# A parallel attention and MLP block: the second layer norm as a factor, memory products with tokens as rows, the memory update on four column tiles, and a new order

## The chip, the cores and the metric

The kernel runs on one core of a Trainium2 chip. The metric is the device time of one execution in microseconds (us). The engines are named as in the profile: PE multiplies matrices and PEld loads their weights, DVE (VectorE), ACT (ScalarE) and POOL (GpSimd) compute elementwise, and SP issues DMAs.

## The reference

For x of 2048 tokens with 512 features the kernel computes x + A(xn) + B(xn), where xn is the layer norm of x. A is an attention with a compressive memory in 32 heads of 16 features; B is an MLP that takes its own layer norm of xn.

```python
xn = layernorm(x)
# A: four segments of 512 tokens; M and z start at zero; phi(t) = t + 1 if t > 0 else exp(t)
for s in range(4):
    p = softmax(qs @ ks.T * 0.25 + mask)
    a_dot = p @ vs
    a_mem = (phi(qs) @ M) / (phi(qs) @ z + 1e-6)
    o_s = g * a_mem + (1 - g) * a_dot       # g = sigmoid(beta), one per head
    M = M + phi(ks).T @ vs
    z = z + phi(ks).sum(tokens)
A = concat(o) @ wo
# B: y is a second layer norm of xn
B = gelu(layernorm(xn) @ w1 + b1) @ w2 + b2      # w1: 512 x 1792, w2: 1792 x 512
```

The mask takes out the keys with a higher index than the query. Because xn has mean zero, the second norm only scales each token: layernorm(xn) is xn times one factor per token, 1/sqrt(var(xn) + 1e-5).

## The kernel before

The work is cut into 16 units i of attention: segment s = i // 4 and a group g = i % 4 of eight heads, whose 8 x 16 features fill the 128 partitions. The MLP is cut into 16 units j: 256 tokens (hf = j // 2) and one half of w1's 14 column blocks (fh = j % 2, FH = 7 blocks). Weights and activations are split into two f16 halves, and a product is three f16 matmuls per 128 rows (`split3`, L499 to 506).

There is no scheduler at run time and none in the compiler that moves work: `streams()` lists the jobs, `ORDER` (L134) is a string in which each letter takes the next job of one stream, and the program issues the jobs in that sequence; each engine then executes its own instructions in order. `BANKS` (L154) gives each product its PSUM bank out of eight. The two strings are written out in the source. The job keys that matter here:

- `X` and `Xt` (L462, L477, L487): load 128-token tiles of x, take the statistics on DVE (`norm_stats`, L424: one inverse root for both norms, `stats[..., 0, :]` for the first and `stats[..., 1, :]` for the first and second in one), normalise on POOL (L458), transpose on PE (L490, four f32 transposes per tile), and split on ACT and DVE (L493, L494) into `xnT`, one buffer for the 512 tokens of a segment.
- `Y` and `Yt`: the same for the MLP's input: x is loaded again, normalised with the second pair of statistics and transposed into `yT`, one buffer of 256 tokens.
- `T`, `Tv`, `Tw`, `Tr`, `N`: projections of k and q for a unit (L521), their low halves, phi on ACT and DVE (L529, L543 to 549), the way through DRAM (stores `kd`, `qd` at L536 to 538, loads into `kst`, `qst` at L557) that brings eight heads into place, and the transposes of phi(k) (L562). `V`: the values (L608).
- `M`, `R`, `Rr`, `S`, `Sg`, `pv`, `PV`: logits and their row maxima (L646, L653; both on 64-row halves of the array), the maxima through DRAM (L664, L669), logits again and exponentials (L688, L695), the causal cut on POOL (L709), and the products with the values on four column tiles of 32 (L722).
- `K` (`kv`, L616): phi(k) transposed times v for a head group as four 128 x 128 f32 products (L621), of which only the diagonal blocks are kept by a mask (L624 or L628) and added to the memory `mst` on POOL (L629).
- `Z`, `Qd`, `Qe`, `Qn`, `Q`: the read from memory, features as rows. `z_rep` spreads z over a 128 x 128 mask (L581), a product with phi(q) of 512 columns gives the denominator of every feature row (L589), ACT adds 1e-6 (L591), the reciprocal is taken by Ln, Exp and a Newton step (L568, L569, L573, L574), a second product of 512 columns gives the numerator (L601), and L602 multiplies them.
- `O`: the attention's division and the sum with the memory part `ame` (L740 to 759). `out`: the product with wo (L849) into `acc`. `st`: the store.
- `D`: one column block of w1 (L781, twelve matmuls of 256 columns on `yT`); each block's product is scaled and gets b1 from ACT or DVE in turn (`Z_ON`, L784, L786). `G`: gelu over all seven blocks in one ACT instruction of 1792 elements (L791). `H`: splitting h in f16 halves (L801, L803, L805). `e`: the product with w2 (L831).
- `wl`, `wm`, `wf`, `ws`: weight loads, sums of squares, scales and splits, all begun in the first 180 us.

## Time and profile before

| what | value |
|---|---|
| median of 3 runs (lowest to highest) | 720.85 us (720.42 to 723.13) |
| the profiled execution's own time | 720.38 us |
| its span in the trace | 718.7 us |
| PE busy | 689.8 us, 5189 matmuls |
| DVE busy | 524.3 us |
| ACT busy | 519.7 us |
| POOL busy | 352.9 us |
| granted PE clock | 1.0 of full speed |

All rows of the trace stand against the span; what lies around it, 720.38 - 718.7 = 1.7 us, is taken as unchanged. An f32 product counts as two matmuls in the rows. The end of a matmul in the trace lies after the start of the next one, since they overlap: the pace of a stretch is read from the start of one group to the start of the next, and not from the busy time alone.

### The profile page before, as it was taken

The numbers are of one execution on the slowest core, as the hardware profiler recorded it, in microseconds if no ns is written. First come the engines' busy times: TensorE is split into PE (matmuls) and PEld (weight loads), VectorE is DVE, ScalarE is ACT, GpSimd is POOL, SyncE is SP. The second block draws the span as 40 slices with busy tenths as digits, with TensorE's granted clock in tenths as the row PEclk, the third lists the DMA queues.
The fourth block names the chain that finished last, engine by engine and source line by source line (L and its number), as shares of the span: only waits on it lengthen the run. The fifth ranks groups of instructions, "written<-read, shape, count | busy, mean of one in ns | idle before, by whom it ended". The sixth has DMA issues, their size and how long they took to land.

```text
span 718.7 us, 14578 instructions
## 1 busy us (share of the span) xinstructions
PE 689.8 (96%) x5189; PEld 379.0 (53%) x5189; DVE 524.3 (73%) x1677; ACT 519.7 (72%) x908; POOL 352.9 (49%) x544
## 2 busy tenths in 40 slices
PE   2799999999999999999999999999999999999997
PEld 2365655564554465665555456556556455455543
DVE  5799877988786659897485866888658484696642
ACT  5989998889767577578936757676864567748980
POOL 3568746655514462654533336445634245334572
PEclk9999999999999999999999999999999999999999
DMA  9886124503220163322313024322240321322101
GB/s 266 242 255 157 53 79 108 127 16 92 52 68 3 61 148 89 82 53 55 96 31 90 16 66 113 92 60 60 68 104 2 97 67 17 82 68 68 32 1 59
DMA packets 54084, 59.16 MB, mean 82 GB/s; under 512 B 5038, under 2 KB 40892, under 8 KB 54012
## 3 DMA queue, kind: packets, MB, share of 16 engines
q1 hardware_dynamic: 51708, 54.04, 27.0%
q0 software_dynamic: 2304, 4.20, 3.6%
q8 instruction: 41, 0.67, 0.4%
q14 instruction: 31, 0.25, 0.1%
HBM read 41.18 MB, written 17.04 MB: 81 GB/s over the span
## 4 chain that ended last, share of the span: by engine, by line
PE 84%; DMA 5%; ACT 5%; DVE 2%; issue 2%; SPq 1%; POOL 0%; POOLq 0%; DVEq 0%; ACTq 0%
PE dense L505 33%; PE dense L831 19%; PE dense L722 9%; PE dense L646 6%; PE dense L688 5%; PE dense L849 5%; DMA qst<-qd 2%; DMA qd<-hl 2%; PE dense L601 2%; PE dense L589 1%; PE dense L621 1%; PE dense L490 1%; ACT pt L695 1%; DMA pt<-in_A_wq_dram 1%; PE dense L562 1%
## 5 line engine op out<-in xcount | busy, mean ns | idle before, releaser
L653 DVE CUSTOM_DVE_ANT_0 dense<-dense,mask 128x384 f32<-128x384 f32 (+3 forms) x512 | 234.0, 524 | 37.9 <-PE dense L646 35.8
L695 ACT ACTIVATE pt<-dense,qkcs 128x512 f32<-128x512 f32 (+1 forms) x384 | 204.4, 628 | 28.0 <-PE dense L688 27.9
L831 PE MATMUL dense<-w2s,hT 128*128 128x512 f16 x672 | 165.3, 380 | 0.0
L505 PE MATMUL dense<-yT,w1s 128*128 128x256 f16 x1344 | 160.5, 273 | 1.8 <-POOL w1s L413 1.4
L709 POOL TENSOR_SCALAR_AFFINE_SELECT pt<-pt 128x256 f32<-128x256 f32 x256 | 102.7, 443 | 104.5 <-ACT pt L695 104.0
L505 PEld LDWEIGHTS <-w1s 128*128 128x128 f16 x1344 | 129.5, 98 | 34.7 <-issue 9.9
L805 POOL TENSOR_TENSOR hT<-hh,hT 128x512 f16<-128x512 f32 x64 | 69.5, 1086 | 64.6 <-ACT hT L803 61.9
L831 PEld LDWEIGHTS <-hT 128*128 128x128 f16 x672 | 60.9, 98 | 71.3 <-issue 16.7
L722 PE MATMUL dense<-pt,vt 128*32 128x512 f32 (+3 forms) x1024 | 76.3, 436 | 0.0
L653 DVE DVE_READ_ACCUMULATOR2_ANT mc<- 128x1 f32 x512 | 71.9, 140 | 0.0
L801 POOL TENSOR_SCALAR hh<-hT,sc 128x512 f32<-128x512 f32 x64 | 43.4, 679 | 46.7 <-ACT hT L791 43.6
L784 ACT ACTIVATE hT<-dense,b1t,sc 128x256 f32<-128x256 f32 x64 | 36.7, 573 | 37.8 <-PE dense L505 37.3
L753 POOL TENSOR_TENSOR nN<-nN,oT 128x512 f32<-128x512 f32 x16 | 20.5, 1280 | 73.8 <-DVE oT L574 73.8
L646 PE MATMUL dense<-kst,qst 48*128 48x384 f16 (+3 forms) x512 | 52.7, 298 | 3.8 <-DMA qst<-qd 3.8
L722 PEld LDWEIGHTS dense<-pt,vt 128*32 128x32 f32 x1024 | 30.9, 109 | 45.2 <-issue 33.4
L688 PE MATMUL dense<-qst,kst 50*128 50x384 f16 (+3 forms) x512 | 52.1, 298 | 2.1 <-DMA qst<-md 1.7
L505 PE MATMUL dense<-xnT,wks 128*128 128x512 f16 x192 | 45.6, 388 | 0.0
L505 PE MATMUL dense<-xnT,wqs 128*128 128x512 f16 x192 | 44.1, 379 | 0.0
L849 PE MATMUL dense<-wos,oT 128*128 128x512 f16 x192 | 43.8, 379 | 0.1
L505 PE MATMUL dense<-wvs,xnT 128*128 128x512 f16 x192 | 43.6, 379 | 0.0
L803 ACT ACTIVATE hT<-hh 128x512 f16<-128x512 f32 x64 | 37.4, 584 | 7.4 <-POOL hh L801 7.4
L786 DVE TENSOR_SCALAR hT<-dense,sc,b1t 128x256 f32<-128x256 f32 x48 | 25.9, 539 | 23.0 <-PE dense L505 22.8
(223 smaller groups left out, 931.5 us busy)
## 6 DMA issues: line engine op xcount, KB each, us to landing
xt<-in_A_x_dram SPq DMA_DIRECT2D x30, 256.0 KB
kd<-hl SPq DMA_DIRECT2D x48, 128.0 KB
qd<-hl SPq DMA_DIRECT2D x48, 128.0 KB
kst<-kd SPq DMA_DIRECT2D x32, 192.0 KB
qst<-qd SPq DMA_DIRECT2D x32, 192.0 KB
acc<-in_A_x_dram SPq DMA_DIRECT2D x16, 256.0 KB
acc<-in_B_b_dram POOLq DMA_DIRECT2D x16, 256.0 KB, 4.1
out_dram<-acc SPq DMA_DIRECT2D x16, 256.0 KB
```

Source lines behind the costliest of these rows:

```text
L505: T.matmul(p, wsl(ws, k, a), xsl(xs, k, b), start=s0 and i == 0, stop=s1 and i == 3 * n - 1)
L646: T.matmul(p[:, o:o + n], stk[i, 0][r, t, P * qb:P * qb + P], stk[i, 1][r, t, :n], start=True, stop=True)
L653: V.tensor_tensor_reduce(p[:, o:o + n], p[:, o:o + n], mask[:, 512 - n:], 1.0, -3e38, OP.add, OP.max, mc[i][:, 4 * b + t, qb:qb + 1])
L688: T.matmul(p[:, o:o + n], stk[i, 1][r, t, P * kb:P * kb + P], stk[i, 0][r, t, P * kb:], start=True, stop=True)
L695: A.activation(pt[i, 4 * b + t][:, OFF[kb]:OFF[kb] + n], p[:, c:c + n], AF.Exp, scale=qkcs[:, 1, i % NG:i % NG + 1])
L709: G.affine_select(v, v, pattern=[[0, 2], [1, P]], compare_op=OP.is_ge, fill=0.0, base=0, channel_multiplier=-1)
L722: T.matmul(p[32 * c:32 * c + 32, P * kb:], vt[s, kb][:, 4 * g + c, 16 * odd:16 * odd + 32], pt[i, 2 * c + odd][:, OFF[kb]:OFF[kb] + LEN[kb ...
L801: G.tensor_scalar(hht[j, c], hz[:, z, :], col(SHH + j % 2), 0.0, op0=OP.mult, op1=OP.add)
L803: A.activation(hT[:, z, 0, :], hht[j, c], AF.Copy)
L805: G.tensor_tensor(hT[:, z, 1, :], hht[j, c], hT[:, z, 0, :], op=OP.subtract)
L831: T.matmul(p, t[:, u, P * a:P * a + P], w2s[:, fo, v, :], start=fi == 0 and n == 0, stop=fi == FH - 1 and n == 2)
L849: T.matmul(p, o[:, u, P * b:P * b + P], wos[:, g, v, :], start=i == 0, stop=i == 3 * NG - 1)
```

## The change

The second norm's pass over x is gone: `Y` and `Yt` fall away, and with them `yT`. The `D` products read `xnT`, which becomes a ring of three halves of 256 tokens; half h of the eight lies in slot h % 3. The factor of each token is computed from the statistics (`ratio`, key `C`), turned into a row with a DVE transpose, written to DRAM by two DMAs, and brought back to all partitions as a row of 256 factors (`ratio_rows`, key `Cb`, a buffer that each half reuses). `D` fills a bank with two column blocks, and one DVE instruction multiplies both by the scale and the row. b1 moves into gelu, which becomes seven ACT instructions with a bias each.

The memory read swaps its operands: phi(q), 128 tokens at a time, is the weight, and the moving operand `mx` has 128 columns of masked memory and eight of z (`z_cols`, key `Z`). The products have tokens as rows and eight denominators per token (`a_mem`, key `Q`); DVE takes an exact reciprocal and multiplies, and four PE transposes and an ACT copy bring the result back to features as rows (`a_turn`, key `Qt`). `gr` holds the gates of all heads on every partition.

`kv` does sixteen products of 32 x 32 instead of four of 128 x 128, on four column tiles, and adds the 32 columns straight to `mst` on DVE, without a mask and without POOL.

In segment 1 the two halves do not lie side by side in the ring (slots 2 and 0), and `T` there takes 24 matmuls of 256 columns instead of twelve of 512 (`x_seg`). `ORDER` and `BANKS` are new throughout; their strings are left out below. The new sequence starts with the x loads ahead of the first weight loads.

```diff
--- before.py
+++ after.py
...
@@ -66,9 +65,9 @@
         for b in range(2):
             put("norm", *[("X", n, b, k) for k in range(4)] * (n > 0))
             put("normt", *[("Xt", n, b, k) for k in range(2)])
-    for n in range(2 * NSEG):
-        put("again", *[("Y", n, 0, k) for k in (0, 2, 3)])
-        put("againt", *[("Yt", n, 0, k) for k in range(2)])
+    for h in range(2 * NSEG):
+        put("ratio", ("C", h))
+        put("ratio2", ("Cb", h))
...
@@ -97,10 +96,8 @@
             put("heads%d" % k, ("O", i, k))
         if s:
             put("mem0", ("Z", i))
-            put("mem1", ("Qd", i))
-            put("mem2", ("Qe", i))
-            put("mem3", ("Qn", i))
-            put("mem4", ("Q", i))
+            put("mem1", ("Q", i))
+            put("mem2", ("Qt", i))
         if s < NSEG - 1:
             put("nat", ("N", i))
             put("kv", ("K", i))
...
@@ -419,7 +416,9 @@
 
     I_MAGIC = 0x5F3759DF
 
-    stats = cst.tile([P, S // P, 2, 2], F32, name="stats")
+    stats = cst.tile([P, 4, 4, 2], F32, name="stats")
+    G.memset(stats, 0.0)
+    nws = {}
 
     def norm_stats(tok, tiles):
 
@@ -430,28 +429,52 @@
             st = sm.tile([P, 6], F32, name="st")
             V.bn_stats(st, t)
             V.bn_aggr(ag[:, j, :], st)
...
-        for j in range(2):
-            V.scalar_tensor_tensor(r[:, :, j, 1], ag[:, :, 0], -1.0, r[:, :, j, 0], op0=OP.mult, op1=OP.mult)
-
-    def norm_apply(tok, tiles, twice, act, j):
+        for o in range(0, n, 2):
+            r = stats[:, (tok + o) // 2 % 4]
+            V.scalar_tensor_tensor(r[:, 1], ag[:, o:o + 2, 0], -1.0, q[:, o:o + 2, 0], op0=OP.mult, op1=OP.mult)
+            V.tensor_copy(r[:, 0], q[:, o:o + 2, 0])
+
+    cd = [dr.tile([2, 4, 32], F32, name=f"cd{h}") for h in range(2 * NSEG)]
+    ct = cst.tile([P, 4, 4, 2], F32, name="ct")
+    cbt = {}
+
+    def ratio(h):
+
+        w, o = nws[2 * h]
+        a, q = w[:, 0, o:o + 2], w[:, 3, o:o + 2]
+        c = stats[:, h % 4, 2]
+        V.tensor_tensor(c, a[:, :, 0], q[:, :, 0], op=OP.mult)
+        V.tensor_tensor(c, c, q[:, :, 1], op=OP.mult)
+        V.transpose(ct.rearrange("p a b c -> p (a b c)"), stats.rearrange("p a b c -> p (a b c)"))
+        j = 8 * (h % 4) + 4
+        for t in range(2):
+            Q.dma_start(cd[h][t], ct.rearrange("(q j) a b c -> j q (a b c)", j=32)[j + t])
+
+    def ratio_rows(h):
+        cbt[h] = sb.tile([P, 256], F32, name="cb")
+        Q.dma_start(cbt[h], bass.AP(tensor=cd[h].tensor, offset=cd[h].offset, ap=[[0, P], [1, 256]]))
+
+    def norm_apply(tok, tiles, act, j):
         for t in tiles[j:j + 1]:
-            a, b = stats[:, tok + j, twice, 0:1], stats[:, tok + j, twice, 1:2]
+            a, b = (stats[:, tok // 2 % 4, k, j:j + 1] for k in range(2))
             if act:
                 A.activation(t, t, AF.Identity, bias=b, scale=a)
             else:
...
@@ -493,22 +509,29 @@
         A.activation(h, p3, AF.Copy, scale=1024.0)
         V.scalar_tensor_tensor(dst[:, :, 1, c0:c0 + P], p3, 1024.0, h, op0=OP.mult, op1=OP.subtract)
 
...
+    def x_seg(s):
+
+        a, b = 2 * s % 3, (2 * s + 1) % 3
+        if b == a + 1:
+            return [(slice(0, 512), lambda k, u: xnT[:, a:a + 2, k, u, :])]
+        return [(slice(256 * j, 256 * j + 256), lambda k, u, h=h: xnT[:, h, k, u, :]) for j, h in enumerate((a, b))]
+
...
     stk, pkn, ame, pqt = {}, {}, {}, {}
-    bg = cst.tile([P, NG, 5], F32, name="bg")
-    mst = cst.tile([P, NG, P], F32, name="mst")
+    bg = cst.tile([P, NG, 4], F32, name="bg")
+    gr = cst.tile([P, H], F32, name="gr")
+    mst = cst.tile([P, NG, 2 * DH], F32, name="mst")
     zst = cst.tile([P, NG], F32, name="zst")
     zs = {}
 
@@ -518,8 +541,8 @@
         s, g = divmod(i, NG)
         w = (wqs, wks)[which]
         p = dense()
-        split3(p, ((w, lambda w, k, a: w[:, g, a, P * k:P * k + P]),
-                   (xnT[s], lambda t, k, a: t[:, k, a, :])), KT, True, True)
+        for c, xs in x_seg(s):
+            split3(p[:, c], lambda k, a: w[:, g, a, P * k:P * k + P], xs)
...
@@ -573,40 +596,49 @@
         V.tensor_tensor(src, src, tmp, op=OP.mult)
         V.scalar_tensor_tensor(dst, src, 2.0, tmp, op0=OP.subtract, op1=OP.mult)
 
-    zrt = {}
-
-    def z_rep(i):
+    amt, mx = {}, {}
+
+    def z_cols(i):
         g = i % NG
-        zrt[i] = sm.tile([P, P], F32, name="zr", bufs=1)
-        V.tensor_scalar(zrt[i], bd.rearrange("p a b -> p (a b)"), zst[:, g:g + 1], None, op0=OP.mult)
-
-    rden = {}
-
-    def a_den(i, part):
-        if part == 0:
-            g = i % NG
-            p = dense()
-            T.matmul(p, zrt[i], pqt[i, 0], start=True, stop=True)
-            rden[i] = sb.tile([P, 512], F32, name="rc")
-            A.activation(rden[i], p, AF.Copy, bias=1e-6, scale=qkcs[:, 0, g:g + 1])
-        elif part == 1:
-            ame[i] = sb.tile([P, 512], F32, name="ame")
-            log_recip(rden[i], ame[i])
-        else:
-            newton(rden[i], rden[i], ame[i])
+        mx[i] = sm.tile([P, P + GH], F32, name="mx")
+        V.tensor_tensor(mx[i][:, :P].rearrange("p (a b) -> p a b", a=4), mst[:, g, :].unsqueeze(1).to_broadcast([P, 4, 2 * DH]),
+                        bd.rearrange("p (a b) c -> p a (b c)", a=4), op=OP.mult)
+        V.tensor_scalar(mx[i][:, P:], half, zst[:, g:g + 1], None, op0=OP.mult)
 
     def a_mem(i):
         g = i % NG
+        amt[i] = sb.tile([P, 512], F32, name="rc")
+        r = sm.tile([P, 4, GH], F32, name="rd", bufs=1)
+        ps = []
+        for b in range(2):
+            p = dense()[:, :2 * (P + GH)].rearrange("p (t c) -> p t c", t=2)
+            ps.append(p)
+            for t in range(2):
+                T.matmul(p[:, t, :], pqt[i, 0][:, P * (2 * b + t):P * (2 * b + t) + P], mx[i],
+                         start=True, stop=True)
+        c = qkcs[:, 0, g:g + 1]
+        for b, p in enumerate(ps):
+            V.tensor_scalar(r[:, 2 * b:2 * b + 2, :], p[:, :, P:], c, 1e-6, op0=OP.mult, op1=OP.add)
+        V.reciprocal(r, r)
+        V.scalar_tensor_tensor(r, r, c, gr[:, GH * g:GH * g + GH].unsqueeze(1).to_broadcast([P, 4, GH]),
+                               op0=OP.mult, op1=OP.mult)
+        for b, p in enumerate(ps):
+            V.tensor_tensor(amt[i][:, 256 * b:256 * b + 256].rearrange("p (t h e) -> p t h e", t=2, h=GH),
+                            p[:, :, :P].rearrange("p t (h e) -> p t h e", h=GH),
+                            r[:, 2 * b:2 * b + 2, :].unsqueeze(3).to_broadcast([P, 2, GH, DH]), op=OP.mult)
+
+    def a_turn(i):
         p = dense()
-        T.matmul(p, mst[:, g, :], pqt[i, 0], start=True, stop=True)
-        V.scalar_tensor_tensor(ame[i], p, bg[:, g, 4:5], rden[i], op0=OP.mult, op1=OP.mult)
+        for t in range(4):
+            T.transpose(p[:, P * t:P * t + P], amt[i][:, P * t:P * t + P], ident)
+        ame[i] = sb.tile([P, 512], F32, name="ame")
+        A.activation(ame[i], p, AF.Copy)
 
...
@@ -617,16 +649,15 @@
         s, g = divmod(i, NG)
         p = dense()
         for b in range(4):
-            v = vt[s, b][:, 4 * g:4 * g + 4, :].rearrange("p a (b c) -> p a b c", b=3)[:, :, 0:3:2, :]
-            T.matmul(p[:, :P], pkn[i][:, b, :], v, start=b == 0, stop=b == 3)
-        m = bd.rearrange("p a b -> p (a b)")
+            for c in range(4):
+                v = vt[s, b][:, 4 * g + c, :].rearrange("p (b c) -> p b c", b=3)[:, 0:3:2, :]
+                T.matmul(p[32 * c:32 * c + 32, :32], pkn[i][:, b, 32 * c:32 * c + 32], v, start=b == 0, stop=b == 3,
+                         tile_position=(0, 32 * c), skip_group_check=True)
         if s == 0:
-            V.tensor_tensor(mst[:, g, :], p[:, :P], m, op=OP.mult)
+            V.tensor_copy(mst[:, g, :], p[:, :32])
             return
         V.tensor_tensor(zst[:, g:g + 1], zs[i], zst[:, g:g + 1], op=OP.add)
-        zr = sm.tile([P, P], F32, name="zr", bufs=1)
-        V.tensor_tensor(zr, p[:, :P], m, op=OP.mult)
-        G.tensor_tensor(mst[:, g, :], mst[:, g, :], zr, op=OP.add)
+        V.tensor_tensor(mst[:, g, :], p[:, :32], mst[:, g, :], op=OP.add)
 
 
     mc = {}
@@ -770,25 +801,25 @@
 
     hzs = [t.rearrange("p f a c -> p f (a c)").bitcast(F32) for t in hTs]
 
-    def d_jobs(j):
+    dp = {}
+
+    def d_job(j, f):
         hf, fh = divmod(j, 2)
-        hz = hzs[fh]
-
-        def f(fi):
-            def go():
-                fo = FH * fh + fi
-                p = dense()
-                split3(p[:, :256], ((WT["1"], lambda w, k, a: w[:, fo, a, P * k:P * k + P]),
-                                    (yT[hf], lambda t, k, a: t[:, k, a, :])), KT, True, True)
-                if Z_ON[fi] == "A":
-                    A.activation(hz[:, fi, :], p[:, :256], AF.Identity, bias=b1t[:, fo:fo + 1], scale=col(CG + fh))
-                else:
-                    V.tensor_scalar(hz[:, fi, :], p[:, :256], col(CG + fh), b1t[:, fo:fo + 1], op0=OP.mult, op1=OP.add)
-            return go
-        return [f(fi) for fi in range(FH)]
+        fo = FH * fh + f
+        if f % 2 == 0:
+            dp[0] = dense()
+        p = dp[0]
+        split3(p[:, 256 * (f % 2):256 * (f % 2) + 256], lambda k, a: WT["1"][:, fo, a, P * k:P * k + P],
+               lambda k, a: xnT[:, hf % 3, k, a, :])
+        if f % 2 or f == FH - 1:
+            f0, n = f - f % 2, 1 + f % 2
+            V.scalar_tensor_tensor(hzs[fh][:, f0:f + 1, :], p[:, :256 * n].rearrange("p (f c) -> p f c", f=n), col(CG + fh),
+                                   cbt[hf].unsqueeze(1).to_broadcast([P, n, 256]), op0=OP.mult, op1=OP.mult)
 
     def gelu(j):
-        A.activation(hzs[j % 2], hzs[j % 2], AF.Gelu_apprx_tanh)
+        for f in range(FH):
+            fo = FH * (j % 2) + f
+            A.activation(hzs[j % 2][:, f, :], hzs[j % 2][:, f, :], AF.Gelu_apprx_tanh, bias=b1t[:, fo:fo + 1])
 
     hht = {}
 
...
```

More of the change, by code (lines that the diff above doesn't have):

```diff
@@ L173, in plan @@
         k = key[0]
-        need = "G" if k == "G" else "E" if k in ("S", "Qe") or k == "O" and key[2] == 1 or k == "T" and (
+        need = "G" if k == "G" else "E" if k == "S" or k == "O" and key[2] == 1 or k == "T" and (
             key[1] >= NG if key[2] == 0 else key[1] < NU - NG) else tab
@@ L432, in norm_stats @@
             V.bn_aggr(ag[:, j, :], st)
-        w = sm.tile([P, 3, 4, 2], F32, name="nw", bufs=1)[:, :, :n]
+        w = sm.tile([P, 4, 4, 2], F32, name="nw", bufs=1)[:, :, :n]
         a, y, b = w[:, 0], w[:, 1], w[:, 2]
-        r = stats[:, tok:tok + n]
+        nws[tok] = w, 0
+        if n == 4:
+            nws[2] = w, 2
+        q = w[:, 3]
         V.tensor_scalar(a[:, :, 0], ag[:, :, 1], EPS, None, op0=OP.add)
@@ L460, in infini_mixer_kernel, with ln @@
     lt = {}
-    def ln(kind, n, b, part):
-        tok = 4 * n + 2 * b if kind == "X" else 2 * n
+    def ln(n, b, part):
+        tok = 4 * n + 2 * b
         if part == 0:
-            lt[kind, n, b] = ts = []
+            lt[n, b] = ts = []
             for j in range(2):
-                name = ("nN", "nD")[j] if (kind, n, b) == ("X", 0, 1) else "xt"
+                name = ("nN", "nD")[j] if (n, b) == (0, 1) else "xt"
                 t = sb.tile([P, D], F32, name=name, bufs=2 if name == "xt" else 1)
@@ L472, in ln, with ln_out @@
         elif part == 1:
-            norm_stats(tok, lt[kind, n, b] + (lt[kind, 0, 1] if n == 0 else []))
+            norm_stats(tok, lt[n, b] + (lt[0, 1] if n == 0 else []))
         else:
-            norm_apply(tok, lt[kind, n, b], kind == "Y", (kind, n, b) == ("X", 0, 1), part - 2)
-    def ln_out(kind, n, b, k):
-        if kind == "X":
-            if n not in xnT:
-                xnT[n] = sb.tile([P, KT, 2, SEG], F16, name="xnT")
-            ln_tr(lt["X", n, b][k], xnT[n], 256 * b + P * k)
-        else:
-            if n not in yT:
-                yT[n] = sb.tile([P, KT, 2, 256], F16, name="yT")
-            ln_tr(lt["Y", n, b][k], yT[n], P * k)
-    def ln_tr(t, dst, c0):
+            norm_apply(tok, lt[n, b], (n, b) == (0, 1), part - 2)
+    xnT = cst.tile([P, 3, KT, 2, 256], F16, name="xnT")
+    def ln_out(n, b, j):
+        t, dst, c0 = lt[n, b][j], xnT[:, (2 * n + b) % 3], P * j
         p = dense()
@@ L494, in ln_tr, with x_cols, split3 @@
         V.scalar_tensor_tensor(dst[:, :, 1, c0:c0 + P], p3, 1024.0, h, op0=OP.mult, op1=OP.subtract)
-    xnT = {}
-    yT = {}
-    def split3(p, parts, n, s0, s1):
-        (ws, wsl), (xs, xsl) = parts
+    def x_seg(s):
[3 more added lines that the diff above has]
+        return [(slice(256 * j, 256 * j + 256), lambda k, u, h=h: xnT[:, h, k, u, :]) for j, h in enumerate((a, b))]
+    def x_cols(s, b, k, u):
+        return xnT[:, (2 * s + b // 2) % 3, k, u, P * (b % 2):P * (b % 2) + P]
+    def split3(p, ws, xs):
         i = 0
-        for k in range(n):
+        for k in range(KT):
             for a, b in ((0, 0), (0, 1), (1, 0)):
-                T.matmul(p, wsl(ws, k, a), xsl(xs, k, b), start=s0 and i == 0, stop=s1 and i == 3 * n - 1)
+                T.matmul(p, ws(k, a), xs(k, b), start=i == 0, stop=i == 3 * KT - 1)
                 i += 1
     stk, pkn, ame, pqt = {}, {}, {}, {}
-    bg = cst.tile([P, NG, 5], F32, name="bg")
-    mst = cst.tile([P, NG, P], F32, name="mst")
+    bg = cst.tile([P, NG, 4], F32, name="bg")
+    gr = cst.tile([P, H], F32, name="gr")
+    mst = cst.tile([P, NG, 2 * DH], F32, name="mst")
     zst = cst.tile([P, NG], F32, name="zst")
@@ L607, in v_nat @@
         p = dense()
-        split3(p, ((xnT[s], lambda t, k, a: t[:, k, a, P * b:P * b + P]),
-                   (wvs, lambda w, k, a: w[:, k, a, :])), KT, True, True)
+        split3(p, lambda k, a: x_cols(s, b, k, a), lambda k, a: wvs[:, k, a, :])
         t = vts[b]
@@ L869, in small_use @@
         V.tensor_reduce(eo, half.rearrange("p (a b) -> p b a", b=2), axis=AX.X, op=OP.max)
+        V.tensor_copy(gr, small["b"][:, :H])
         t = small["b"][:, :H].rearrange("p (g a) -> p g a", a=GH)
@@ L875, in gates @@
     def gates():
+        A.activation(gr, gr, AF.Exp, scale=-1.0)
+        V.tensor_scalar(gr, gr, 1.0, None, op0=OP.add)
+        V.reciprocal(gr, gr)
         e = sm.tile([P, NG], F32, name="be")
```

63 lines of the change are left out of this document (29 added, 34 removed).

## The prediction

> **What bounds the kernel now.** I read the page's busy times first, then the stretches, PE's waits, and PE's timeline in the middle, where the rate of the steady state shows.
>
> ```profile
> span 718.7 us, 14578 instructions
> PE 689.8 (96%) x5189; PEld 379.0 (53%) x5189; DVE 524.3 (73%) x1677; ACT 519.7 (72%) x908; POOL 352.9 (49%) x544
> ...
> PEclk9999999999999999999999999999999999999999
> ```
>
> PE is busy for 96% of the span at the full granted clock; no other engine passes 73%. The stretches (length, then busy us of PE, PEld, DVE, ACT, POOL) say where the 28.9 us of PE's idle time are:
>
> ```profile
> 0.00:14.00 14.00, 1.04 (x4) 0.98 (x5) 6.54 (x29) 6.34 (x15) 6.71 (x20) 1.00 0.89 258
> 14.00:45.00 31.00, 24.55 (x149) 16.25 (x149) 25.28 (x86) 27.85 (x50) 17.66 (x18) 1.00 0.79 232
> 100.00:550.00 450.00, 448.62 (x3450) 247.38 (x3449) 340.25 (x1106) 325.55 (x569) 215.92 (x341) 1.00 0.28 72
> 550.00:700.00 150.00, 145.86 (x1101) 76.90 (x1099) 96.18 (x271) 106.57 (x184) 70.67 (x114) 1.00 0.21 52
> ```
>
> The start loses 12.96 + 6.45 = 19.4 us, the 450 us of the middle 1.4 us, the stretch from 550 to 700 us 4.1 us. In PE's list of waits the two longest single ones are both at the start:
>
> ```profile
> PE dense L490 <- POOL xt L458: 7.4, 1, 7.4
> PE dense L359 <- ACT wqs L343: 6.4, 2, 5.6
> ```
>
> So outside the start a microsecond of PE work taken out is a microsecond of time, provided that nothing else becomes late. Busy time alone would not show how much work a group is, because matmuls overlap; I use the distance from one group's start to the next one's. PE's timeline (start, us, what):
>
> ```profile
> 456.19 1.02 PE L589 MATMUL dense<-phq,zr 128*128 128x512 f32 x2
> 457.05 1.47 PE L505 MATMUL dense<-yT,w1s 128*128 128x256 f16 x12
> 458.36 1.46 PE L831 MATMUL dense<-w2s,hT 128*128 128x512 f16 x6
> ...
> 461.07 1.02 PE L601 MATMUL dense<-phq,mst 128*128 128x512 f32 x2
> 461.94 2.10 PE L831 MATMUL dense<-w2s,hT 128*128 128x512 f16 x9
> 463.88 2.75 PE L505 MATMUL dense<-xnT,wqs 128*128 128x512 f16 x12
> 466.47 1.46 PE L831 MATMUL dense<-w2s,hT 128*128 128x512 f16 x6
> 467.76 1.47 PE L505 MATMUL dense<-yT,w1s 128*128 128x256 f16 x12
> 469.17 0.61 PE L688 MATMUL dense<-qst,kst 50*128 50x512 f16 x6
> ...
> 473.84 1.05 PE L621 MATMUL dense<-vt,pkn 128*128 128x128 f32 x8
> 474.73 0.49 PE L505 MATMUL dense<-yT,w1s 128*128 128x256 f16 x3
> ```
>
> ```profile
> 110.99 0.60 PE L562 MATMUL dense<-ident,phk 128*128 128x128 f32 x4
> 111.43 0.82 PE L505 MATMUL dense<-yT,w1s 128*128 128x256 f16 x6
> ```
>
> From start to start the denominator's product takes 457.05 - 456.19 = 0.86 us, the numerator's 0.87, the memory update 0.89, four f32 transposes 0.44. A `D` job takes 1.31 before another full-array group, but 469.17 - 467.76 = 1.41 before a group on 64-row halves: a change of the array's tiling costs 0.10 us.
>
> **PE's work, part by part.** Removed:
> - `Y`'s transposes: 16 tiles x 0.44 = 7.0 us.
> - Denominator and numerator in twelve units: 12 x 0.86 + 12 x 0.87 = 10.3 + 10.4 us.
> - The old memory update: 12 x 0.89 = 10.7 us. Together 38.4 us.
>
> Added:
> - The new read: four products of 136 columns, two passes each. The old update is eight passes of 128 columns with new 128 x 128 f32 weights each, the same form: 0.89 x 136/128 = 0.95, x 12 = 11.4 us.
> - `Qt`: four transposes, 0.44 x 12 = 5.3 us.
> - The update on four column tiles: sixteen products of 32 columns, two passes each, on tiles that the value products already use:
>
> ```profile
> 78.61 0.64 PE L722 MATMUL dense<-pt,vt 128*32 128x512 f32 x4
> 78.61 0.14 PEld L722 LDWEIGHTS dense<-pt,vt 128*32 128x32 f32 x5 [0.21 <-issue]
> 115.42 2.36 PE L722 MATMUL dense<-pt,vt 128*32 128x512 f32 x32
> 117.71 0.39 PE L688 MATMUL dense<-qst,kst 50*128 50x512 f16 x2
> ```
>
> Four matmuls on four tiles fill 0.64 us, where two passes of that width on the full array fill 1.02 (L589 above): they run beside each other. The 32 of one block are eight rounds of four with 320 columns in the mean, and take 2.29 us, 0.10 of it the change of tiling: 0.27 us a round, 0.86 ns a column. Eight rounds of 32 columns would be 0.22 us. That is one end. The other end: no matmul of the trace is so short, and the next round's weights may not arrive while this round runs. The loads last about 0.11 us (five, nearly together, 0.14), which gives 8 x (0.11 + 0.027) = 1.1 us. I take 0.3, near the lower end, because loads and matmuls of the value products start nearly together: 12 x 0.3 = 3.6 us (2.6 to 13.2).
> - Changes of tiling: counted along the two order strings, 266 before and 277 after; the new `K` mostly stands next to `pv`, already on column tiles. 11 x 0.10 = 1.1 us.
> - Segment 1's projections in half-width pieces: two `D` jobs, 24 of 256 columns, take 2 x 1.31 = 2.62, a projection 466.47 - 463.88 = 2.59; eight of them, 0.2 us.
>
> Together 21.6 us; net 38.4 - 21.6 = 16.8 us less PE work.
>
> One rule of the Trainium skill speaks against the column tiles: TensorEngine Tiling (Array Packing), Instruction Overhead, says that a matmul has some 60 cycles of overhead, that one column costs as much as 60, and that a tiling factor should not come out of a dimension that is small already. At the 25 ns that the Trainium skill gives for these 60 cycles (TensorE: Matmul & The Clock Gate, Back-to-back issue gap), 32 matmuls would be 0.8 us as an estimate, 9.6 us for twelve units, and the sum would be 10.8 us instead of 16.8. Four value matmuls that start almost at once speak against counting it once per tile; no row here shows it for 32 columns.
>
> **The start.** SP issues in order, and `xt` and the weights go through it:
>
> ```profile
> 0.82 0.45 SPq L284 DMA_DIRECT2D wks<-in_A_wk_dram  x1
> 1.33 0.49 SPq L284 DMA_DIRECT2D wqs<-in_A_wq_dram  x1
> ...
> 14.72 1.16 SPq L470 DMA_DIRECT2D xt<-in_A_x_dram  x2
> ```
>
> ```profile
> 24.76 0.60 ACT L493 ACTIVATE yT<-dense 128x512 f16<-128x512 f32 x1
> ```
>
> With x first in the queue, the normalisation that ends PE's 7.4 us wait starts up to about 1 us earlier. `Y`'s load, 1.16 us of issue ahead of w1's, goes, and so do two copies of 0.6 us on an ACT that is 90% busy from 14 to 45 us. Against that, DVE gets some more small instructions in the statistics, and wk and wq come after four loads. Bounds: 3 us gained (1 + 1.2 + 1.2, less a little) to 1 us lost. I take 1.5 gained. `Y`'s first eight transposes (0.9 of the 16.8) lie in this stretch and are worth nothing beside that, so the start adds 0.6.
>
> **Off the path.** ACT and DVE:
>
> ```profile
> L784 ACT ACTIVATE hT<-dense,b1t,sc 128x256 f32<-128x256 f32 x64 | 36.7, 573 | 37.8 <-PE dense L505 37.3
> L791 ACT ACTIVATE hT<-hT 128x1792 f32<-128x1792 f32 x16 | 27.2, 1698 | 0.2
> L695 ACT ACTIVATE pt<-dense,qkcs 128x256 f32<-128x256 f32 x128 | 50.6, 496 | 1.7 <-PE dense L688 1.7
> ```
>
> Seven gelu pieces at about 0.5 us are 3.5 instead of 1.7, 29 us more in sixteen units, but 36.7 us of bias and scale leave ACT, as do the Ln and Exp of the denominators. DVE loses the Newton step, the masks and its share of the blocks, and gets the paired scaling, the reciprocals and the products by rows: about even. POOL loses work. With DVE and ACT at 340 and 326 of the middle's 450 us these cost nothing; without that cover the 1.8 us of each longer gelu would cost 29. The second products `e` begin at least 11 us of PE work after their gelu in the new order (its letters, added up with the paces above), so that cover holds.
>
> The new waits are on SP: `Cb` waits for the ratio's store and, since there is one row buffer, for the last DVE scaling of the half before. Stores of k and q, loads of the maxima and x loads queue behind it. At nothing, since the order has between 4 and 15 us of PE work from each `Cb` to the end of the first pair that needs it; the price without that cover is in the third rival. The ring makes `Xt` wait for the last reader of the slot: in the new order at least 32 us of PE work lie between them.
>
> **The sum.** 720.4 (the profiled execution) - 16.8 - 0.6 = 703.0 us. It stands 0.5 us below the median of the runs, so against 720.85 this is -2.5%. About 0.5%, or 3.6 us, is what a measurement of this kernel can tell from no change.
>
> **Rivals.**
> 1. Short matmuls don't overlap on the column tiles (weights waited for each round): 1.1 instead of 0.3 per update, 720.4 - 7.2 - 0.6 = 712.6 us. For it: 32 columns are far below any f32 form of the middle. Chance 0.12. By the Trainium skill's floor of the tiling page above it would be 709 us.
> 2. The new order has more stalls. The chain of waits shows one of the old order, where DVE's small work for the maxima stood behind an output product:
>
> ```profile
> 589.98 2.56 issue
> 593.50 1.41 DMA md<-mhl
> 594.92 1.69 DMA qst<-md
> ```
>
> It put 2.6 us into the chain. With less PE work between the same round trips, four more such places would give 703 + 10 = 713 us. For it: every queue is rearranged. Against it: the old order had 1.4 us idle in 450. Chance 0.12.
> 3. Slower: `Cb` blocks SP. The row comes by a load after a store, as the maxima do, 1.41 + 1.69 = 3.1 us; if it takes that time with nothing to cover it, DVE stands before the pair's scaling, the banks stay full, and PE stops for 3.1 us in each of seven halves: 703 + 22 = 725 us. It decides only where the row comes later than the 4 to 15 us of PE work that the order leaves. Chance 0.05.
> 4. The start loses the gain, or DVE's row products take the place of PE's saving here and there, and 717 to 724 remains: 0.05.
>
> **How the numbers follow.** The forecast, 697 to 709, has the remaining 0.66: low with 0.22 per update, 3 us gained at the start and 3 us of the 4.1 idle gone (697); high with 6 us of new small stalls. Rivals 1 and 2 reach to 713. 697 to 713 holds about 0.82. Faster by over 0.5% is the forecast, the first rival and most of the second: 0.88. Within 0.5%: 0.07. Slower: 0.05.
>
> **What would show it.** Right: PE's busy time falls by about 17 us or more and its idle time stays below 30 us; `kv`'s block, start to start, is near 0.3 us and the new read near 0.95; PE's first transposes start before 13.5 us; DVE stays near 520 us of busy time. Wrong: `kv` at 1 us (rival 1); new rows above 3 us in PE's list of waits after 50 us (rival 2); waits of DVE on the row `cb`, or of SP before it with PE idle at the same time (rival 3).

## The result, and the profile after

The changed kernel takes 704.20 us (median of 4 runs, 704.07 to 706.84), the kernel before in the same session 721.69 (4 runs, 720.42 to 723.13): a ratio of 0.9766, 95% interval 0.9734 to 0.9797. The forecast was 703.0, with 697 to 713 as its range. The profiled execution took 704.33 us. Its page, span and busy times:

```profile
span 702.3 us, 15520 instructions
PE 674.0 (96%) x5605; PEld 382.6 (54%) x5605; DVE 535.5 (76%) x1753; ACT 485.8 (69%) x901; POOL 335.5 (48%) x521
```

PE's busy time fell by 15.8 us (689.8 to 674.0) and its idle time by 0.6 (28.9 to 28.3). Where the idle time lies has changed much more than its sum. The stretches of the changed kernel (length, then busy us of PE, PEld, DVE, ACT, POOL, the granted clock, DMA share, GB/s):

```profile
0.00:14.00 14.00, 2.79 (x13) 2.70 (x14) 8.59 (x36) 7.01 (x15) 8.91 (x23) 1.00 0.94 268
14.00:45.00 31.00, 25.48 (x151) 15.68 (x150) 26.52 (x82) 28.92 (x51) 12.87 (x13) 1.00 0.91 241
45.00:100.00 55.00, 53.23 (x456) 28.50 (x455) 51.77 (x190) 48.03 (x96) 38.36 (x49) 1.00 0.47 126
100.00:550.00 450.00, 444.19 (x3871) 257.95 (x3869) 356.41 (x1168) 303.01 (x562) 204.84 (x324) 1.00 0.26 67
550.00:690.00 140.00, 140.00 (x1084) 74.20 (x1082) 89.23 (x278) 98.84 (x182) 70.39 (x114) 1.00 0.19 48
```

The first 45 us lose 16.7 us where they lost 19.4, the stretch to 100 us 1.8 where it lost almost nothing, the middle 5.8 instead of 1.4, and the 140 us after that none, where 550 to 700 us had lost 4.1. PE's list of waits names the new one:

```profile
PE dense L356 <- ACT wqs L340: 11.4, 2, 9.0
PE dense L527 <- DVE mc L684: 4.8, 1, 4.8
PE dense L506 <- POOL xt L481: 2.2, 1, 2.2
PE dense L373 <- ACT w1s L340: 1.4, 1, 1.4
PE dense L527 <- POOL w1s L410: 1.4, 1, 1.4
```

The second row is one wait of 4.8 us at 118 us. It is of the kind that the forecast said would count against it: over 3 us, after 50 us. PE's new groups (busy, mean ns of one, idle before them):

```profile
L617 PE MATMUL dense<-mx,phq 128*128 128x136 f32 x96 | 13.3, 282 | 0.0
L633 PE MATMUL dense<-ident,rc 128*128 128x128 f32 x48 | 7.3, 275 | 0.0
L654 PE MATMUL dense<-vt,pkn 128*32 128x32 f32 x384 | 5.7, 198 | 0.0
```

and one memory update and what follows it, from PE's timeline:

```profile
113.04 0.46 PE L654 MATMUL dense<-vt,pkn 128*32 128x32 f32 x32
113.32 2.38 PE L753 MATMUL dense<-pt,vt 128*32 128x512 f32 x32
```

The 32 passes of 32 columns take 0.28 us from start to start. Added up from start to start over all twelve units, the update is 3.6 us, the new read 11.6 and `Qt` 5.7, against the 3.6, 11.4 and 5.3 of the forecast.

### The profile page after: what moved, and what is told of

Same layout as the page of the kernel before. It is cut to its first block, busy times and chain, and to the rows that moved or that the text cites. A ratio compares the mean times of both kernels' runs of the same rounds, so it can differ in the third digit from the quotient of the medians.

```text
span 702.3 us, 15520 instructions
## 1 busy us (share of the span) xinstructions
PE 674.0 (96%) x5605; PEld 382.6 (54%) x5605; DVE 535.5 (76%) x1753; ACT 485.8 (69%) x901; POOL 335.5 (48%) x521
## 4 chain that ended last, share of the span: by engine, by line
PE 86%; DVE 6%; DMA 2%; issue 2%; ACT 2%; POOL 0%; SPq 0%; POOLq 0%; DVEq 0%; ACTq 0%
PE dense L527 35%; PE dense L862 19%; PE dense L753 10%; PE dense L880 6%; PE dense L719 5%; PE dense L677 5%; DVE dense L684 2%; PE dense L617 2%; PE dense L506 1%; DMA qst<-qd 1%; PE dense L633 1%; DMA w2s<-in_B_w_dram 1%; PE dense L585 1%; ACT pt L726 1%; DVE wvs L404 1%
## 5 line engine op out<-in xcount | busy, mean ns | idle before, releaser
L684 DVE CUSTOM_DVE_ANT_0 dense<-dense,mask 128x384 f32<-128x384 f32 (+3 forms) x512 | 234.1, 523 | 28.2 <-PE dense L677 27.7
L527 PE MATMUL dense<-xnT,w1s 128*128 128x256 f16 x1344 | 162.9, 274 | 6.6 <-DVE mc L684 4.8
L862 PE MATMUL dense<-w2s,hT 128*128 128x512 f16 x672 | 167.1, 380 | 0.0
L740 POOL TENSOR_SCALAR_AFFINE_SELECT pt<-pt 128x256 f32<-128x256 f32 x256 | 99.4, 420 | 135.6 <-ACT pt L726 135.2
L836 POOL TENSOR_TENSOR hT<-hh,hT 128x512 f16<-128x512 f32 x64 | 67.9, 1061 | 78.5 <-ACT hT L834 76.8
L753 PE MATMUL dense<-pt,vt 128*32 128x512 f32 (+3 forms) x1024 | 78.0, 436 | 0.0
L684 DVE DVE_READ_ACCUMULATOR2_ANT mc<- 128x1 f32 x512 | 71.4, 139 | 0.0
L816 DVE SCALAR_TENSOR_TENSOR hT<-dense,sc,cb 128x512 f32<-128x512 f32 x64 | 43.3, 679 | 30.3 <-PE dense L527 25.8
L822 ACT ACTIVATE hT<-hT,b1t 128x256 f32<-128x256 f32 x112 | 46.8, 496 | 4.4 <-DVE hT L816 4.3
L527 PE MATMUL dense<-xnT,wks 128*128 128x512 f16 (+1 forms) x240 | 46.7, 349 | 0.0
L527 PE MATMUL dense<-xnT,wqs 128*128 128x512 f16 (+1 forms) x240 | 44.2, 337 | 0.0
```

The costliest lines, as they stand in the source:

```text
L527: T.matmul(p, ws(k, a), xs(k, b), start=i == 0, stop=i == 3 * KT - 1)
L684: V.tensor_tensor_reduce(p[:, o:o + n], p[:, o:o + n], mask[:, 512 - n:], 1.0, -3e38, OP.add, OP.max, mc[i][:, 4 * b + t, qb:qb + 1])
L740: G.affine_select(v, v, pattern=[[0, 2], [1, P]], compare_op=OP.is_ge, fill=0.0, base=0, channel_multiplier=-1)
L753: T.matmul(p[32 * c:32 * c + 32, P * kb:], vt[s, kb][:, 4 * g + c, 16 * odd:16 * odd + 32], pt[i, 2 * c + odd][:, OFF[kb]:OFF[kb] + LEN[kb ...
L822: A.activation(hzs[j % 2][:, f, :], hzs[j % 2][:, f, :], AF.Gelu_apprx_tanh, bias=b1t[:, fo:fo + 1])
L836: G.tensor_tensor(hT[:, z, 1, :], hht[j, c], hT[:, z, 0, :], op=OP.subtract)
```

## The experiments

### The changed kernel again, and the one long wait

What stands in front of the 4.8 us wait is this, in the timeline of the changed kernel (start, us, what; the bracket is idle time and who ended it):

```profile
115.41 0.87 POOL L844 DMA_DIRECT2D acc<-in_B_b_dram  x1
115.73 0.18 DVE L657 COPY mst<-dense 128x32 f32<-128x32 f32 x1
115.83 5.86 DVE L404 SCALAR_TENSOR_TENSOR w2s<-oT,sc,w2s 128x512 f16<-128x512 f32 x1
116.05 1.42 POOL L410 TENSOR_TENSOR w2s<-w2s 128x512 f16<-128x512 f32 x1
117.17 1.40 POOL L836 TENSOR_TENSOR hT<-hh,hT 128x512 f16<-128x512 f32 x1
...
118.31 0.93 POOL L406 TENSOR_SCALAR oT<-oT,sc 128x512 f32<-128x512 f32 x1
119.00 0.98 POOL L481 TENSOR_SCALAR xt<-xt,stats 128x512 f32<-128x512 f32 x1
119.72 0.97 POOL L740 TENSOR_SCALAR_AFFINE_SELECT pt<-pt 128x256 f32<-128x256 f32 x2
120.47 0.67 POOL L832 TENSOR_SCALAR hh<-hT,sc 128x256 f32<-128x256 f32 x1
121.61 0.55 DVE L684 CUSTOM_DVE_ANT_0 dense<-dense,mask 128x384 f32<-128x384 f32 x1
...
123.03 2.67 PE L527 MATMUL dense<-xnT,w1s 128*128 128x256 f16 x12 [4.85 <-DVE mc L684]
```

DVE makes the low half of piece 5 of w2's second half (L404, an STT: scalar_tensor_tensor). The others of this line take 0.73 to 1.7 us; this one stands for 5.86, from 115.83 to 121.69. All that while GpSimd runs one instruction after the other, each starting before the one ahead has ended; the last ends at 121.14, and the STT 0.55 us later. Behind the STT in DVE's queue are the maxima (L684), which give back the banks that PE's next `D` needs.

> The changed kernel once more, unchanged, to see whether its one long stall comes again. In the first trace one DVE instruction (the low half of the sixth block of w2's second half, two inputs in SBUF) lasts 5.9 us instead of 0.75 and PE then waits 4.8 us for DVE. Theory port: it stands behind an unbroken run of POOL instructions, which the fixed order makes, so it comes again at the same place with 4 to 6 us. Rival chance: it was one execution's mishap, and the instruction lasts 0.7 to 1.7 us here. Time by either: 704 to 705 us, since the four times known lie close together.

Measured: 704.33 us (6 runs, 703.36 to 706.45), ratio 0.978 (0.976 to 0.981). The STT took 5.86 us again and PE waited 4.9. So it is no accident of one execution.

### The STT given to GpSimd

```
 if SPLIT[m][n] == "V":
     A.activation(h, r, AF.Copy, scale=s)
-    V.scalar_tensor_tensor(l, r, s, h, op0=OP.mult, op1=OP.subtract)
+    if m == "2b" and n == 5:
+        G.tensor_scalar(r, r, s, 0.0, op0=OP.mult, op1=OP.add)
+        G.tensor_tensor(l, r, h, op=OP.subtract)
+    else:
+        V.scalar_tensor_tensor(l, r, s, h, op0=OP.mult, op1=OP.subtract)
```

> The low half of that one block is computed by two POOL instructions in place of the one DVE instruction; the same values. Theory port: DVE no longer waits behind POOL's run at this place, PE's 4.8 us of waiting go, and the time falls by 3.5 to 5 us, to about 700. Rival data: DVE waited for the block's data or for ACT's half, so POOL waits as long and all behind it too, and the time stays at 704 or rises. Rival passed on: the stall goes but the next wait takes its place, 702 to 704.

Measured: 697.12 us (695.79 to 698.49), ratio 0.967 (0.965 to 0.970): 7.2 us less than the changed kernel in the same session, more than the wait itself and than expected. The rest is the clock. Two stretches of 4 us right behind the wait, first in the changed kernel, then in this one (the last three numbers: granted clock, DMA share, GB/s):

```profile
121.00:125.00 4.00, 1.97 (x10) 1.45 (x10) 3.76 (x17) 0.00 (x0) 0.14 (x1) 0.77 0.00 0
125.00:129.00 4.00, 4.00 (x23) 1.61 (x22) 3.19 (x12) 2.08 (x4) 0.22 (x1) 0.81 0.00 0
```

```profile
121.00:125.00 4.00, 4.00 (x27) 1.66 (x25) 2.43 (x12) 3.07 (x7) 3.97 (x7) 1.00 0.02 4
125.00:129.00 4.00, 4.00 (x37) 2.14 (x39) 3.25 (x9) 3.97 (x8) 2.31 (x6) 1.00 0.31 98
```

The changed kernel had a clock of 0.77 and 0.81 there, which is 4 x 0.23 + 4 x 0.19 = 1.7 us of lost time, as much as 3.4 us at half the clock. Without the wait the clock stays at 1.00. So the wait cost about 4.9 + 1.7 = 6.6 us of the 7.2. The Trainium skill (TensorE: Matmul & The Clock Gate, What's actually happening) says that the clock falls to half after an idle window and that this window is 3413 ns long. The trace agrees in the length: 1.7 us is half of such a window. It doesn't bear out that PE must stand idle for all of it: in the run with the update on the whole array (below) the clock is 0.85 and 0.73 in these two stretches, 4 x 0.15 + 4 x 0.27 = 1.7 us again, behind a wait of 2.3 us.

### Once more beside the STT moved, and GpSimd's run made longer

Three runs on one chip. In the first the STT stays on DVE, with its operands, and was to come some 9 us earlier, with ACT's half of the piece:

```
-        CALL[key[0]](*key[1:])
+        if key != ("ws", "2b", 5, 0):
+            CALL[key[0]](*key[1:])
+        if key == ("O", 0, 1):
+            w_split("2b", 5, 0)
```

> The same STT of the same operands stays on DVE, but it and ACT's half of the piece come some 9 us earlier, after the first output product of that stretch, at about 106.5 us, where GpSimd has nothing to do from 106.3 to 108.7. Theory port: the STT takes 0.75 to 1.6 us, PE's wait on mc goes, and the time falls as it did when the STT was given to GpSimd, to 696.5 to 699. Rival (its operands): it takes 5.9 us again, now at 106.5; PE waits then for the maxima or for DVE's products there, and the time stays at 702 to 705.

Measured: 699.53 us (697.59 to 700.92), ratio 0.971 (0.968 to 0.975). Its timeline:

```profile
109.83 0.75 DVE L404 SCALAR_TENSOR_TENSOR w2s<-oT,sc,w2s 128x512 f16<-128x512 f32 x1 [1.06 <-ACT w2s L403]
...
112.66 1.26 POOL L784 TENSOR_TENSOR nN<-nN,oT 128x512 f32<-128x512 f32 x1 [4.17 <-DVE fa L377]
```

It ran 6 us earlier, at 109.83 us. There GpSimd stood idle for 4 us, and the same instruction takes 0.75 us. Its operands are not the cause; its place is.

> The kernel of the run in which GpSimd does the low half of piece 5, once more, beside the moved one on the same chip. It was 697.1 us (0.967 of the time before). Expected again: 696 to 699, no window of half the granted clock between 121 and 129 us, and within 1.5 us of the moved one if the cause is only that DVE stood behind GpSimd.

Measured: 697.49 us (696.01 to 698.95), ratio 0.969 (0.966 to 0.972). The two are 2.0 us apart, where within 1.5 was expected, but their intervals overlap. The changed kernel did not run on this chip; by the ratio to the kernel before (0.978 for it) both are faster. Giving the STT to GpSimd is the fastest version seen, twice.

In the third, GpSimd computes the piece of L410 three times in a row inside its run:

```
-            G.tensor_tensor(l, r, h, op=OP.subtract)
+            for _ in range(3 if (m, n) == ("2b", 4) else 1):
+                G.tensor_tensor(l, r, h, op=OP.subtract)
```

> GpSimd computes the low half of piece 4 of w2 three times instead of once, inside the unbroken run of GpSimd instructions during which DVE's STT of piece 5 stands for 5.86 us; the result is the same. Start to start in that run this instruction takes 1.12 us beside the STT. Theory port (an STT with two SBUF operands is not served until GpSimd stops): the STT grows by 2 x 1.1 to 2 x 1.4 = 2.2 to 2.8 us, to 8.1 to 8.7, PE's wait on mc from 4.8 to 7 to 7.6, and the time by 2 to 3 us over the changed kernel (704.3), to 706 to 707.5. Rival (the STT is slow for a reason of its own, its operands or where they lie): it stays at 5.86 us, PE's wait at 4.8, and the time at 704.3.

Measured: 698.45 us (697.66 to 701.08), ratio 0.971 (0.968 to 0.974): more work on GpSimd made it faster. Both expectations missed.

```profile
117.04 2.20 DVE L404 SCALAR_TENSOR_TENSOR w2s<-oT,sc,w2s 128x512 f16<-128x512 f32 x1
...
117.26 4.22 POOL L411 TENSOR_TENSOR w2s<-w2s 128x512 f16<-128x512 f32 x3
```

The first of the three took 1.42 us and ended at 118.68. The STT ended at 119.24, 0.56 us behind it and long before GpSimd was done with the three: it was let in between two of them. So it does not wait for GpSimd to stop. To see whether the repetition on the same tile had opened the way, the two extra ones were put behind instructions on other tiles:

```
         CALL[key[0]](*key[1:])
+        if key in (("H", 1, 2, 2), ("X", 1, 0, 2)):
+            w_split("2b", 4, 2)
```

> GpSimd's low half of piece 4 is computed three times again, but the two extra ones no longer stand right behind the first: one stands behind the subtraction that makes hT, one behind the normalisation of x, so each follows an instruction on another tile. In the run before, the three stood in a row on one tile, and DVE's STT ended 1.5 us after the first of them had its 1.4 us, 2.2 us in all instead of 5.86. Theory gap (the STT is let in only where GpSimd's instructions leave a gap; an instruction that follows one on another tile starts before that one has ended and leaves none, one that writes the same tile again does): the run is unbroken and 2 x 1.12 us longer, so the STT takes 7.9 to 8.3 us, PE's wait on mc 6.8 to 7.3, and the time is 706 to 708 us. Rival (more instructions of GpSimd at that place let the STT in, however they are ordered): the STT takes 2 to 4 us, and the time is 698 to 701.

Measured: 705.07 us (5 runs, 700.89 to 706.26), ratio 0.979 (0.977 to 0.981), less than 1 us from the changed kernel and between the two expectations. The profiled execution was the fastest of the five (700.89), so it may not stand for the others:

```profile
114.64 5.06 DVE L404 SCALAR_TENSOR_TENSOR w2s<-oT,sc,w2s 128x512 f16<-128x512 f32 x1
...
118.23 0.93 POOL L406 TENSOR_SCALAR oT<-oT,sc 128x512 f32<-128x512 f32 x1
118.91 1.40 POOL L481 TENSOR_SCALAR xt<-xt,stats 128x512 f32<-128x512 f32 x1
120.15 1.27 POOL L410 TENSOR_TENSOR w2s<-w2s 128x512 f16<-128x512 f32 x1
```

Here the STT took 5.06 us and ended at 119.70, inside L481, although an instruction on another tile stood ahead of that. L481 took 1.40 us instead of the 0.98 of the changed kernel: now GpSimd was held up by DVE (as in the run with the update on the whole array, below, where L481 took 1.39 us and the STT ended inside it). The theory of the gap fails in this form. In each of these traces the STT ends 0.54 to 0.57 us behind the end of a GpSimd instruction: 121.69 behind 121.14 in the changed kernel, 119.24 behind 118.68, here 119.70 behind L406's end at 119.16, and 122.65 behind L406's end at 122.08 in the run with the update on the whole array. What the runs show together: the STT is slow only while GpSimd runs, it is let in at one of the borders between GpSimd's instructions, and whoever is in holds up the other. Which border lets it in is open: L406's end let it in in two traces and not in the changed kernel, where L406 ends at 119.24.

### Parts of the change, one at a time

The first two runs have the changed kernel beside them (704.33). The others were run on a chip where it was not; there the ratio to the kernel before is to be compared with the changed kernel's 0.977 and 0.978.

**The memory update on the whole array again** (eight passes of 128 columns, four DVE additions of the blocks on the diagonal):

```
...
-                T.matmul(p[32 * c:32 * c + 32, :32], pkn[i][:, b, 32 * c:32 * c + 32], v, start=b == 0, stop=b == 3,
-                         tile_position=(0, 32 * c), skip_group_check=True)
+            T.matmul(p[:, :P], pkn[i][:, b, :], v, start=b == 0, stop=b == 3)
...
```

> The memory update's products back on the full array, four of 128 columns per unit instead of sixteen of 32 on column tiles; memory kept in 32 columns, so DVE takes the diagonal blocks by four small adds per unit. Theory PE work: 0.89 instead of 0.30 us per unit is +7.1 us, and 15 more changes of tiling (the update stands between value products in most units) at 0.10 are +1.5: about 8.6 us slower, 712 to 714. Rival relief: the update's worth lay in the mask and in POOL's add that went, and PE's part is mostly hidden: less than 3 us slower.

Measured: 712.44 us (709.28 to 714.34), ratio 0.988 (0.985 to 0.991), 8.1 us more than the changed kernel beside it. One update on PE's timeline:

```profile
115.91 1.16 PE L653 MATMUL dense<-vt,pkn 128*128 128x128 f32 x8
117.00 2.36 PE L754 MATMUL dense<-pt,vt 128*32 128x512 f32 x32
```

1.09 us from start to start in place of 0.28; 12 x 0.81 = 9.7 us, of which 8.1 arrive. The STT was let in after 3.24 us in this run and PE waited 2.3 us for it instead of 4.9, which gives some of it back.

**`Qt` twice** (the four transposes repeated):

```
-        for t in range(4):
+        for t in (0, 1, 2, 3, 0, 1, 2, 3):
             T.transpose(p[:, P * t:P * t + P], amt[i][:, P * t:P * t + P], ident)
```

> The four transposes that turn the memory part back are done twice per unit, 48 more f32 transposes spread over the middle, with the same result. Theory PE work: 48 x 0.11 = 5.3 us slower, 709 to 710. Rival slack: the new order leaves PE idle here and there (6.2 us more between 45 and 550 us than the old one), part of the work fits in, and it is 0 to 3 us slower.

Measured: 710.21 us (707.26 to 711.33), ratio 0.985 (0.983 to 0.988), 5.9 us more: what PE gets in added work, 48 x 0.11 = 5.3 us, comes out as time, all of it.

**One gelu instead of seven** (leaves out the bias b1):

```
-        for f in range(FH):
-            fo = FH * (j % 2) + f
-            A.activation(hzs[j % 2][:, f, :], hzs[j % 2][:, f, :], AF.Gelu_apprx_tanh, bias=b1t[:, fo:fo + 1])
+        A.activation(hzs[j % 2], hzs[j % 2], AF.Gelu_apprx_tanh)
```

> Gelu as one ACT instruction of 1792 elements again; this leaves out the bias b1. The seven pieces cost ACT 2.9 us per unit where one instruction cost 1.7, so ACT loses about 19 us of work. Theory PE work: ACT is covered, the time changes by less than 1 us. Rival ACT: the longer gelu delays what stands behind it on ACT, and the kernel gets 2 us or more faster.

Measured: 708.46 us (705.81 to 710.05), ratio 0.982 (0.979 to 0.985). ACT's busy time is 467.0 us, 18.8 less, and the time is not lower. So the rival fails: the pieces of gelu cost no time that this run shows. That the time changes by less than 1 us is not borne out either; the ratio is higher than the changed kernel's, with intervals that just touch, and why isn't settled. In the profiled execution, the fastest of the four (705.81), the clock behind the long wait was 0.60 and 0.55 in the two stretches of 4 us (4 x 0.40 + 4 x 0.45 = 3.4 us instead of 1.7); the other three have no trace.

**The ratio's row loaded twice**, which keeps SP longer at each `Cb`:

```
-        Q.dma_start(cbt[h], bass.AP(tensor=cd[h].tensor, offset=cd[h].offset, ap=[[0, P], [1, 256]]))
+        for _ in range(2):
+            Q.dma_start(cbt[h], bass.AP(tensor=cd[h].tensor, offset=cd[h].offset, ap=[[0, P], [1, 256]]))
```

> The row of factors is loaded twice into its buffer, the second load after the first has landed, so SP stands about 2 us longer before its next DMA at each of the eight places, and the row is there later. Theory PE work: the 4 to 15 us of PE work after each load cover it, less than 1 us. Rival SP (the third of the prediction): the row's way over DRAM is on the path, and it is 5 to 16 us slower.

Measured: 708.31 us (707.18 to 711.26), ratio 0.983 (0.980 to 0.985). SP's waits, and the second stretch:

```profile
SPq L474 <- DMA cb<-cd: 22.9, 8, 4.2
```

```profile
14.00:45.00 31.00, 22.39 (x136) 13.56 (x134) 25.84 (x78) 28.58 (x50) 12.70 (x12) 0.94 0.90 237
```

SP stood 22.9 us more, in eight places of up to 4.2 us. Behind the first of them, at 25 us, PE is busy 3.1 us less by 45 us (22.39 instead of 25.48), with a wait of 1.4 us for w2's squares and one of 1.5 for `qst` that the changed kernel has not. The other seven cost PE some 2 us in the middle (7.8 us idle from 100 to 550 us instead of 5.8). The time, about 4 us more, lies between the two expectations: most of the 22.9 us is covered, but not at the start, and less than 1 us was too little. The profiled execution (711.23) is one of the two slowest.

**The first weights of q and k ahead of x** in SP's order:

```
-    "ggaaeePPeegaaeRaPeRaReeaebebQRbbRRcQRSVVSSSehXfiXVdeX1ljXmeYYZWY0WYZ1ylk0YGZGk1YeGGY0WmT2GGZo0W3ToG2eUHIAoJ42o"
+    "ggeaaePPeegaaeRaPeRaReeaebebQRbbRRcQRSVVSSSehXfiXVdeX1ljXmeYYZWY0WYZ1ylk0YGZGk1YeGGY0WmT2GGZo0W3ToG2eUHIAoJ42o"
```

> One letter moved: the first weight loads (wk and wq of the first group) are issued ahead of the first x loads, as in the old order, all else as changed. Theory start: the norm's chain begins about 1 us later and PE's first group with it, 0.5 to 1.5 us slower. Rival weights: the chain through the weights' squares, scales and splits is as late as the norm's, so that it is within 0.5 us or a little faster.

Measured: 707.32 us (705.54 to 709.74), ratio 0.981 (0.978 to 0.984). PE's waits:

```profile
PE dense L506 <- POOL xt L481: 8.0, 1, 8.0
PE dense L356 <- ACT wqs L340: 7.9, 2, 5.5
```

The two rows hold 15.9 us, where the changed kernel has 11.4 + 2.2 = 13.6. The order of the loads decides which of the two waits is long, and x first is the better by 2 to 3 us, more than the 0.5 to 1.5 that was expected.

**PE kept busy before the first projection** (twelve dummy f32 products):

```
         p = dense()
+        for _ in range(12 if g0 else 0):
+            T.matmul(p[:, P:2 * P], ones, ident, start=True, stop=True)
```

> Twelve more f32 products of 128 columns, whose results are never read, in the gap before PE's first projection (15.4 to 17.8 us). In the trace that projection takes 5.2 us from start to start instead of 2.6, and the same one took 4.0 us before the change. Theory cold: PE runs slowly after the idle start, and work put into the gap brings the projection near 2.6 us; what follows at the start is bound by ACT and by w1's splits, so that 0.5 to 2 us of it come out in the time. Rival operands: the projection waits for its operands piece by piece and stays at 5.2 us; no change or slower by up to 2 us.

Measured: 704.24 us (703.66 to 704.66), ratio 0.976 (0.974 to 0.978).

```profile
19.08 2.75 PE L529 MATMUL dense<-xnT,wks 128*128 128x512 f16 x12
...
26.59 0.38 PE L375 MATMUL dense<-am,ones 128*128 128x2 f32 x2 [1.67 <-ACT w1s L340]
...
28.27 4.13 PE L529 MATMUL dense<-xnT,wqs 128*128 128x512 f16 x12
```

The projection took 2.75 us instead of 5.28 and ended 1.7 us sooner (21.83 against 23.56). So PE was slow there and its operands were in time: the theory holds for the projection. The row of the granted clock doesn't tell it, it reads 1.00 at that place in both. But the 0.5 to 2 us do not come out in the time. Up to w1's squares the lead stays (26.59 against 28.32). Then this run has a stretch at half the clock (0.50 from 28 to 30 us) in which q's next projection takes 4.13 us, where the changed kernel takes 2.75. At 44 us 0.8 us is left (the values' products begin at 43.57 against 44.38), and between 45 and 100 us PE stands idle 0.5 us more. What binds that stretch, the loads or ACT, no run here shows.

## Why the prediction was right, step by step

- **PE's work**: -16.8 us forecast, -15.8 measured. The measured one holds 1.7 us of the half clock behind the wait; the run that gave the STT to GpSimd a second time has no such stretch in its middle, and its PE is busy for 673.3 us, -16.5. The parts hold as well: 0.28 to 0.30 us for an update (0.3), 0.97 for a read (0.95), 5.7 for `Qt` (5.3). Undoing the update cost 8.1 us, doubling `Qt` 5.9. No run puts `Y`'s transposes or the old read back; that their 7.0 and 20.7 us are right is borne out by the total alone.
- **Rival 1** (short products don't overlap on column tiles) fails: 32 passes in 0.28 us are 9 ns each. The Trainium skill's overhead for every matmul (TensorEngine Tiling (Array Packing), Instruction Overhead), by which it would have been 709 us, is not seen across column tiles. The forecast's choice of 0.3 rested on the value products; its reason on the other side, that no matmul of the trace is so short, misread the trace, which has f32 products of one and two columns at the start (L376, L378), though not on column tiles.
- **The start**: 0.6 us beside the 16.8 was forecast; PE's idle time up to 100 us fell by 1.0 (19.4 to 16.7, and 0.0 to 1.8). The first transposes came at 11.77 us, before 13.5 as said. But what x gained, the weights lost: the wait for their squares grew from 6.4 to 11.4 us, and the two waits together went only from 13.8 to 13.6.
- **Off the path**: ACT fell to 485.8 us, and the gelu pieces cost nothing. DVE was said to stay near 520 us and rose to 535.5, 5.1 of it the one STT. With the STT on GpSimd DVE is busy for 529.7 us and PE's waits for DVE are 0.8 us in all: the sum of DVE's work had room, the place of one instruction had not.
- **`Cb` and SP** (rival 3): no wait of DVE on `cb` in the list of waits. SP does wait there, 46.6 us before the ratio's stores and 14.0 before the row's loads, but the waits of PE that could hang on it, those for `qst`, are 0.9 us in three places. A doubled row cost PE 3.1 us at the start and some 2 in the middle.
- **New stalls** (rival 2): the forecast gave 12 in 100 to four of them at 2.6 us, 10 us in all. One came and cost 6.6. The mechanism that the prediction pointed to was named wrongly, too. It put the old 2.6 us down to DVE's small work standing behind an output product; in DVE's timeline of before, the 2.56 us at 589.98 lie inside one instruction of the old `z` path, 128 columns that take 3.83 us while GpSimd runs without a break from 588.34 to 592.53, as the STT takes 5.86:

```profile
588.79 3.83 DVE L581 TENSOR_SCALAR zr<-bd,zst 128x128 f32<-128x128 f32 x1
```

The sum had left the idle time after 550 us standing. PE's waits of before in that stretch are these:

```profile
PE dense L688 <- DMA qst<-md: 1.7, 1, 1.7
PE dense L646 <- DMA qst<-qd: 1.6, 2, 1.1
```

The first hangs on that instruction, which the change takes out; the second has gone as well in the new order. All of the 4.1 us went; no run took apart which edit did what.

So the mechanism was right, PE's work costed from start to start, but that the total is right within 1.3 us (704.33 against 703.0) is in part luck: 6.6 us of a stall that the new order makes stand against 4.1 us of waits that go with the change. The 2.5 us between them shrink to 1.3 by smaller differences that no run separates. With the one STT given to GpSimd the changed kernel gains 22 to 24 us (719.56 - 697.49 and 720.89 - 697.12).

## What to carry to other kernels

When PE is busy for 96% and its work is costed from start to start, a sum of the parts can be good to half a microsecond, as it was here in seventeen; what it can't see are single stalls. So look in the timeline for a DVE instruction that takes several times its usual duration while GpSimd runs without a break: move it by a few places or give it to GpSimd. And count a long PE wait with the slow clock behind it: after the start, every wait of 2.3 us or more had one here, at 1.7 us, in two runs at 3.4.
